# Attention and a squared-ReLU MLP on one core: the second half's output products regrouped by Strassen's scheme, with channels on the partitions

## Chip, cores and metric

One core of a Trainium2 chip. The metric is the device time of one execution in microseconds (us). All data is float32; inputs and outputs lie in DRAM.

## What is computed

Causal attention (4 batches, 12 heads, 448 positions, head width 64) gives x with 4 x 448 = 1792 tokens and 768 channels. Then follows an MLP without gates:

```
x   = softmax(mask(q k^T / 8)) v            # 1792 tokens x 768 channels
h   = max(x @ w_in, 0)                      # 768 -> 2048
out = (h * h) @ w_out                       # 2048 -> 768
```

The weights arrive as 8-byte floats and are turned into float32 on the chip.

## The kernel before

**Precision.** Every float32 factor is split into a high part `hi` (a copy in the format that TensorE reads) and a low part `lo = value - hi`. A product is three matmuls into one PSUM bank: hi*hi, hi*lo, lo*hi. A split is thus two instructions: `hi` by POOL or ACT (L305, L290), `lo` by DVE or POOL (L293, L297).

**Two phases.** Tokens 0 to 895 (batches 0 and 1) go first, tokens 896 to 1791 second. The attention of batches 0 and 1 opens the kernel; that of batches 2 and 3 is woven into phase 0's matmuls. In each phase the 2048 hidden channels come in 4 groups of 4 x 128. A group has an **h stage** (x @ w_in, ReLU, square) and an **o stage** (times w_out, added to an accumulator). In phase 0 the h stage is plain. Phase 0 loads the raw weights (`piece`), turns them into float32, splits them into the tiles `wi` and `wo`, and stores float32 copies in DRAM (`wz_dram` and `wo_dram`; `keep` also stores hi and lo of w_in for groups 0 and 3).

**Phase 1.** The h stage goes by Strassen's scheme with seven products (Winograd's form): the 896 tokens, the 768 channels and 256 hidden channels are each halved. `w_parts` loads the quarters of the weights, makes the sums s1 to s4 on DVE or POOL and splits them; `h_pair` runs 7 products x 3 channel blocks x 3 matmuls of 448 columns for each pair of hidden blocks (two pairs per group). The sums of x (t1 to t4) were put in DRAM by `spill` and come back by `x_part`. The o stage is plain (`o_unit`): tokens on the PSUM partitions, 14 units (7 token blocks x 2 column halves) of 4 x 3 matmuls of 384 columns, and one DVE addition each into `acc`. For groups 2, 1 and 0 `fetch` reads w_out back from `wo_dram` and splits it; group 3's is still there from phase 0. The groups go 3, 2, 1, 0 in phase 1; in the last one each unit of `acc` is stored as it is done.

**Order of the work.** A planner (`Plan.emit`) lists all operations with estimated costs and starts, at each step, the one that can start earliest; each operation names the engines that may do it, with a `BIAS` in us against some. What comes out is a fixed order for each engine: PE, ACT, DVE, POOL, and the DMA queue of SP. Each of them runs strictly in that order, so an instruction that waits holds up everything behind it on its engine. Buffers are pools (`plan.pool`): `f` for float32 scratch, `w` for split weights of phase 1, `r` for hidden values, `ps` for the eight PSUM banks. `lend` makes other tiles part of a pool once their first use is over.

Lines that matter below: L804 to L806 the plain o stage's matmuls, L743 to L747 the h stage's of phase 1, L616 to L618 of phase 0, L820 the addition into `acc` (issued by L293), L823 the store of the result.

Of the kernel before, what the change touches and what calls it, by code (L numbers as in the profile page):

```python
# [20 lines left out]
class Op:  # L21
    __slots__ = ("rank", "ways", "then", "left", "ready", "take", "drop", "lag")
# [14 lines left out]
class Plan:  # L37
# [8 lines left out]
    BIAS = {PE: 0.0, ACT: 0.5, DVE: 1.0, POOL: 0.0, DMA: 0.0, DMA2: 0.0}  # L46

    def __init__(self):
        self.ops, self.writer, self.readers = [], {}, {}
        self.pools, self.caps, self.held = {}, {}, {}  # L50

# [45 lines left out]
    def emit(self):  # L97
# [72 lines left out]
def kernel(  # L170
# [51 lines left out]
    NRAW, NZ, NB, NR = 3, 3, 1, 6  # L222
    CB = NP // 2
# [20 lines left out]
    def tiles(nm, n, shape, dtype, pool=const):  # L244
# [17 lines left out]
    plan.pool("r", tiles("r", NR, [P, S], F32), r=2, xs=4, y=6)  # L262
    plan.pool("f", [], fz=5, s=3, xp=3, fo=2)
    spare = [whole[:, i * S:(i + 1) * S].bitcast(F32) for i in range((2 * NRAW + NZ + NB) * PCW // S)]
    lent_f = plan.lend("f", spare)
# [4 lines left out]
        for i in range(2 * GF)] + [lambda i=i: late["w"][i] for i in range(2)])  # L270
# [4 lines left out]
    plan.pool("ps", tiles("ps", 8, [P, 512], F32, psum), mm=2, sc=4, pt=2, av=1, st=5)  # L275
# [23 lines left out]
    pool_too = [True]  # L299

    def two_sources(*args):
        return [on_dve(*args, 0.03) + SHARED] + ([on_pool(*args)] if pool_too[0] else [])
# [5 lines left out]
    def split(rank, n, hi, lo, src, reads, key, after=(), drop=(), take=None):  # L308
# [3 lines left out]
        plan.op(rank, two_sources(n, lo, src, lambda: hi().bitcast(F32), ALU.subtract),  # L312
                list(reads) + [(key, 0)], [(key, 1)], after, drop=drop)
# [162 lines left out]
    def spill(n, av, at):  # L476
# [27 lines left out]
        elif second:  # L504
# [6 lines left out]
            less(x12, [av])  # L511
# [13 lines left out]
    wo_dram = nc.dram_tensor("wo_whole", (NG, 2 * GF, P, CH), F32, kind="Internal").ap()  # L525

# [9 lines left out]

    def fetch(rank, gr, a, ch):
        h = Hold("f", "fo")
        plan.op(rank - 6, [(DMA, 0.9, lambda: nc.sync.dma_start(
            out=h.t[:, :CH], in_=wo_dram[gr, a + GF * ch]))], [("wod", gr, a, ch)], [h], take=h)  # L540
        cols = slice(ch * CH, (ch + 1) * CH)
        split(rank - 2, CH, lambda: late["wo"][:, 0, a, cols], lambda: late["wo"][:, 1, a, cols],
              lambda: h.t[:, :CH], [h], ("wo", a, ch), drop=[h])
# [3 lines left out]
    def piece(rank, kind, gr, a, ch, after):  # L547
# [88 lines left out]
    SEVEN = ("11", "s2", "12", "s3", "s1", "22", "s4")  # L636
# [21 lines left out]
    ahead = []  # L658

    def w_parts(gr, u, rank, last):  # L660
# [36 lines left out]
        else:  # L697
            for m, (key, f, j) in enumerate((("21", 1, 0), ("22", 1, 1), ("11", 0, 0), ("12", 0, 1))):
                Z[key] = h = Hold("f", "fz")
                plan.op(rank - 10 + m, [(DMA, 0.7, lambda h=h, f=f, j=j: nc.sync.dma_start(  # L700
                    out=h.t[:, :CBW].rearrange("p (c n) -> p c n", n=P), in_=wz_dram[gr, 2 * u + f, j]))],
                    [("wzd", gr, CB * j + c) for c in range(CB)], [h], gate, take=h)
        Z["s1"], Z["s2"], Z["s4"] = Hold("f", "s"), Hold("f", "s"), Hold("f", "s")
        Z["s3"] = Z["21"]

        def done(key):
            W[key] = w = Hold("w", "w")
            split(at(key), CBW, lambda: flat(w.t[:, 0]), lambda: flat(w.t[:, 1]), lambda: Z[key].t[:, :CBW],
                  [Z[key]], w, (), [Z[key]], take=w)

        def made(key, a, b, op, drop):
            combine(rank, CBW, Z[key], Z[a], Z[b], op, [Z[a], Z[b]], [Z[key]],
                    take=Z[key] if key != "s3" else None, drop=[Z[d] for d in drop])
        def direct(key):
            if gr not in (0, NG - 1):
                done(key)
        direct("11")
        made("s1", "21", "22", ALU.add, ("22",))
        made("s2", "s1", "11", ALU.subtract, ("s1", "11"))
        done("s2")  # L720
        direct("12")
        made("s3", "11", "21", ALU.subtract, ("11",))
        done("s3")
        done("s1")
        direct("22")
        made("s4", "12", "s2", ALU.subtract, ("12", "s2"))
        done("s4")
        ahead[:] = plan.ops[-2:]
        return W

    def h_pair(u, W, rank, step):

# [35 lines left out]
        product("s2", "b", True)  # L768
        add("u2", "b", "u2", False, [bank["b"]])
# [3 lines left out]
        squared(f1, 0, y["11"], rank)  # L773
        product("s3", "d", True)
        add("u3", "d", "u2", True, [])
        product("s1", "c", True)
        add("u3", "c", "u3", False, [])
        relu("u3")
        squared(f2, 1, y["u3"], rank)
# [3 lines left out]
        squared(f2, 0, y["21"], rank)  # L783
# [3 lines left out]
        squared(f1, 1, y["12"], rank)  # L787
        return rank

    def o_unit(ph, gr, t, ch, rank, step, after):  # L790
# [23 lines left out]
        first, final = (0, NG - 1) if ph == 0 else (NG - 1, 0)  # L814
        if gr == first:
# [14 lines left out]
    stack = ExitStack()  # L830
# [13 lines left out]
    def group(ph, gr, rank, step, begin):  # L844
# [7 lines left out]
        else:  # L852
            mid = (begin + rank) / 2
            W = [w_parts(gr, 0, begin, mid), w_parts(gr, 1, mid, rank)]
# [11 lines left out]
        else:  # L866
            for u in range(2):
                rank = h_pair(u, W[u], rank, H_US * step)
        for i in range(2 * GF):
            at = begin + (rank - begin) * (i + 0.5) / 8  # L870
            if ph == 0:
                piece(at, "o", gr, i % GF, i // GF, swap)
            elif gr < NG - 1:
                fetch(at, gr, i % GF, i // GF)
        begin = rank
        for ch in range(2):
            for t in range(NT):
                rank = o_unit(ph, gr, t, ch, rank, O_US * step, swap)
# [14 lines left out]
    def replace():  # L893
# [3 lines left out]
        late["w"] = tiles("w2_", 2, [P, 2, CB, P], F32R, pool)  # L897

    attended = over(plan.ops[mark:], lent_w[2 * GF:], replace)
    over(pieces, lent_f)  # L900
    entered = over(h_ops, lent_w[:2 * GF])
    keys = [(OTHER[key], i) for key in SEVEN for i in range(CB)]
    pool_too[0] = False
# [3 lines left out]
    for ph in range(1, NPH):  # L907
        for gr in range(NG - 1, -1, -1):
# [34 lines left out]
```

## Time and profile before

| | us |
|---|---|
| three runs | 624.04, 625.79, 626.65 |
| median | 625.79 |
| the profiled execution's own time | 624.94 |
| its span, first to last instruction | 623.2 |
| phase 1, from its first h matmul (at 399.21) | 224.0 of the span |

The profile is of one execution. "Busy" is the time in which an engine ran an instruction; matmuls overlap, so the distance between the starts of matmuls tells more than the duration of one. PEld is the loading of weights, which runs beside the matmuls. The granted clock is a share of TensorE's 2.4 GHz.

### The profile page before, as it was taken

What the parts mean: (1) busy time and instruction counts of PE and PEld (TensorE: products, weight loads), DVE (VectorE), ACT (ScalarE), POOL (GpSimd) and SP (SyncE); (2) the same over time, 40 slices, a digit from 0 to 9 for tenths busy, and PEclk for the clock granted to TensorE, in tenths of its full rate; (3) what the DMA queues carried; (4) which work ended last, traced back from release to release, by engine and by line L of the source; (5) the groups of instructions that cost most, each with busy time, mean ns of one, the idle gap of its engine ahead of it and who ended that gap; (6) DMA issues with size and microseconds to landing.
All of it is one profiled execution on the core that took longest, in us unless ns stands there. A gap on an engine that the chain in (4) does not pass through costs nothing.

```text
span 623.2 us, 11325 instructions
## 1 busy us (share of the span) xinstructions
PE 601.2 (96%) x3864; PEld 528.9 (85%) x3864; DVE 410.9 (66%) x932; ACT 306.0 (49%) x768; POOL 312.0 (50%) x427
## 2 busy tenths in 40 slices
PE   3989999999999999999999999999999999999997
PEld 2656677789988898888898889999999999999997
DVE  5779866478774789765977517886159646845432
ACT  4778987768667747585466540043235004202400
POOL 1457784568788756876655653452135222213100
PEclk9899999999999999999999999999999999999999
DMA  8888844689895679676875529832121203310022
GB/s 149 169 202 152 168 121 73 144 271 251 214 220 178 161 220 251 179 196 201 234 199 182 171 82 345 265 106 74 50 64 52 63 14 102 122 57 1 1 90 88
DMA packets 166314, 91.68 MB, mean 147 GB/s; under 512 B 115440, under 2 KB 157552, under 8 KB 166256
## 3 DMA queue, kind: packets, MB, share of 16 engines
q1 hardware_dynamic: 162544, 90.50, 54.1%
q10 hardware_dynamic: 3712, 0.46, 0.5%
q8 instruction: 30, 0.49, 0.3%
q14 instruction: 28, 0.23, 0.1%
HBM read 64.19 MB, written 26.74 MB: 146 GB/s over the span
## 4 chain that ended last, share of the span: by engine, by line
PE 83%; DVE 6%; DMA 4%; ACT 3%; POOL 1%; issue 1%; SPq 0%; ACTq 0%; DVEq 0%; POOLq 0%
PE ps L804 12%; PE ps L806 12%; PE ps L805 11%; PE ps L616 6%; PE ps L427 6%; PE ps L617 6%; PE ps L618 6%; PE ps L407 5%; PE ps L743 5%; PE ps L745 5%; PE ps L747 5%; PE ps L367 4%; DVE ps L380 2%; ACT ap L384 1%; POOL ap L393 1%
## 5 line engine op out<-in xcount | busy, mean ns | idle before, releaser
L804 PE MATMUL ps<-wo,g 128*128 128x384 f32 x448 | 151.7, 339 | 0.0
L806 PE MATMUL ps<-wo,g 128*128 128x384 f32 x448 | 150.1, 335 | 1.1 <-DVE g L293 1.1
L805 PE MATMUL ps<-wo,g 128*128 128x384 f32 x448 | 149.9, 335 | 0.0
L393 POOL TENSOR_SCALAR ap<-ap,asm 128x128 f32<-128x128 f32 (+6 forms) x122 | 78.2, 660 | 50.4 <-DVE asm L452 29.3
L290 ACT ACTIVATE r<-ps 128x448 f32<-128x448 f32 x60 | 32.7, 547 | 139.1 <-PE ps L747 108.4
L290 ACT ACTIVATE words<-words 128x384 f32<-128x384 f32 (+3 forms) x112 | 66.7, 613 | 52.0 <-DVE words L293 10.9
L806 PEld LDWEIGHTS ps<-wo,g 128*128 128x128 f32 x448 | 84.1, 188 | 1.4 <-DVE g L293 1.4
L804 PEld LDWEIGHTS ps<-wo,g 128*128 128x128 f32 x448 | 84.1, 188 | 1.3 <-issue 0.8
L805 PEld LDWEIGHTS ps<-wo,g 128*128 128x128 f32 x448 | 84.1, 188 | 0.2
L293 DVE TENSOR_TENSOR acc<-ps,acc 128x384 f32<-128x384 f32 x84 | 46.3, 554 | 55.7 <-PE ps L806 55.3
L380 DVE CUSTOM_DVE_ANT_0 ps<-ps,mask 128x448 f32<-128x448 f32 (+6 forms) x168 | 68.6, 444 | 18.9 <-PE ps L367 10.1
L616 PE MATMUL ps<-x,wi 128*128 128x448 f32 x192 | 74.8, 390 | 1.2 <-ACT x L290 0.6
L305 POOL TENSOR_SCALAR wo<-words 128x384 fp32r<-128x384 f32 x44 | 27.1, 621 | 88.1 <-PE ps L806 66.0
L617 PE MATMUL ps<-x,wi 128*128 128x448 f32 x192 | 70.2, 366 | 0.2 <-DVE x L293 0.2
L618 PE MATMUL ps<-x,wi 128*128 128x448 f32 x192 | 70.1, 365 | 0.0
L384 ACT ACTIVATE ap<-ps,mx 128x448 f32<-128x448 f32 (+6 forms) x126 | 58.3, 481 | 10.3 <-DVE mx L380 8.3
L305 POOL TENSOR_SCALAR g<-r 128x448 fp32r<-128x448 f32 x50 | 32.0, 642 | 53.5 <-ACT r L290 52.8
L290 ACT ACTIVATE r<-r 128x448 f32<-128x448 f32 x75 | 43.2, 578 | 30.0 <-DVE r L293 28.7
L293 DVE CUSTOM_DVE_ANT_0 words<-words 128x768 uint16<-128x768 uint16 (+1 forms) x56 | 45.4, 810 | 13.5 <-ACT words L290 10.5
L305 POOL TENSOR_SCALAR wi<-words 128x384 fp32r<-128x384 f32 (+1 forms) x43 | 28.0, 654 | 44.2 <-DVE words L585 15.4
L743 PE MATMUL ps<-x,wi 128*128 128x448 f32 x135 | 49.6, 368 | 0.4 <-DVE r L293 0.4
L745 PE MATMUL ps<-x,wi 128*128 128x448 f32 x135 | 49.5, 367 | 0.0
(83 smaller groups left out, 1139.5 us busy)
## 6 DMA issues: line engine op xcount, KB each, us to landing
words<-in_moe_w_in_dram SPq DMA_DIRECT2D x24, 512.0 KB, 4.6
words<-in_moe_w_out_dram SPq DMA_DIRECT2D x32, 384.0 KB, 3.8
wi_split<-wi SPq DMA_DIRECT2D x24, 256.0 KB, 3.6
out_dram<-acc SPq DMA_DIRECT2D x28, 192.0 KB, 3.2
v<-in_v_dram SPq DMA_DIRECT2D x24, 192.0 KB, 3.9
wo_whole<-words SPq DMA_DIRECT2D x24, 192.0 KB, 4.2
wi_whole<-words SPq DMA_DIRECT2D x18, 256.0 KB, 4.5
words<-wi_whole SPq DMA_DIRECT2D x24, 192.0 KB, 2.8
```

Source lines behind the costliest of these rows:

```text
L290: return (ACT, t_act(n, psum, more), lambda: nc.scalar.activation(dst(), src(), func, **kw))
L293: return (DVE, t_dve(n) + more, lambda: nc.vector.tensor_tensor(out=dst(), in0=a(), in1=b(), op=op))
L305: return (POOL, t_pool(n), lambda: nc.gpsimd.tensor_scalar(dst(), src(), 1.0, 1.0, op0=ALU.mult, op1=ALU.mult))
L380: plan.op(at, [(DVE, t_dve(w), lambda: nc.vector.tensor_tensor_reduce(out=at_(), in0=at_(), in1=mask[:, S - w:], scale=-SCALE, scalar=3.0e ...
L393: (POOL, 0.00083 * CW[c] + 0.3, lambda: nc.gpsimd.tensor_scalar(*operands(), 1.0, op0=ALU.mult, op1=ALU.mult)),
L616: nc.tensor.matmul(o, w[:, 0], x[:, 0], start=c == 0, stop=False)
L617: nc.tensor.matmul(o, w[:, 0], x[:, 1], start=False, stop=False)
L618: nc.tensor.matmul(o, w[:, 1], x[:, 0], start=False, stop=c == NP - 1)
L743: nc.tensor.matmul(o, w.t[:, 0, c], x[:, 0], start=begin and c == 0, stop=False, skip_group_check=True)
L804: nc.tensor.matmul(res(), g[:, 0], w[:, 0], start=f == 0, stop=False)
L805: nc.tensor.matmul(res(), g[:, 0], w[:, 1], start=False, stop=False)
L806: nc.tensor.matmul(res(), g[:, 1], w[:, 0], start=False, stop=f == GF - 1)
```

## The change

The o stage of phase 1 is turned: output channels lie on the PSUM partitions and 448 tokens are the columns. For the groups 0, 3 and 2, which come first (the order is now 0, 3, 2, 1), it uses the seven products; group 1, the last, is plain in the turned form. For this:

- `h_pair` makes the sums of the squared hidden values (t1 to t4) and splits seven factors instead of four per pair, into tiles of pool `g7` (12 tiles). Its products come in another order (11, 12, s3, s1, s2, 22, s4). ReLU and square are on ACT alone, a factor's `lo` on DVE alone.
- 15 running sums of 128 x 448 (`late["sum"]`) take the place of `acc`; the last group adds its product, transposes 32 x 32 blocks on DVE and stores the result in pieces of 32 channels (128 bytes) by four DMAs per tile, from SP or ACT.
- The sums of weights (s1 to s4, for the o stage of the three groups, and for the h stage of the groups 3, 2, 1) are made by DMAs that add: `added_up` loads a quarter, and POOL issues DMAs that add others onto it, with copies that change the sign in between, on POOL or ACT. The h stage of group 0 still adds on DVE or POOL.
- Phase 0 stores `wo` for all four groups (32 instead of 24 stores of 192 KB), and hi and lo of 26 of the 32 pieces in `wh_dram` (384 KB each).
- When phase 0 and the attention are over, the memory of `wo` and `acc` is used for g7, sums and scratch (`grow`). The pool `w` has 9 tiles instead of 10 and now serves both stages. From then on the bias against DVE is 0.3 instead of 1.0, against ACT 0 instead of 0.5, and POOL may again do operations with two sources.

```diff
-    BIAS = {PE: 0.0, ACT: 0.5, DVE: 1.0, POOL: 0.0, DMA: 0.0, DMA2: 0.0}
+    FEW = {PE: 0.0, ACT: 0.5, DVE: 1.0, POOL: 0.0, DMA: 0.0, DMA2: 0.0}
+    MANY = {PE: 0.0, ACT: 0.0, DVE: 0.3, POOL: 0.0, DMA: 0.0, DMA2: 0.0}
...
+    HWAY, OWAY, GWAY = slice(None), slice(1, 2), slice(0, 1)
+    TURNS, LEAD = (0, 3, 2, 1), 9
...
-    plan.pool("f", [], fz=5, s=3, xp=3, fo=2)
+    plan.pool("f", [], fz=5, xp=3, oz=12, tr=3)
...
-        if kind == "o" and gr < NG - 1:
+        if kind == "o":
             plan.op(rank, [(DMA, 0.8, lambda: nc.sync.dma_start(out=wo_dram[gr, a + GF * ch], in_=zf()))],
                     [zt], [("wod", gr, a, ch)], drop=[zt])
+            if (a % 2, ch) != (0, 1) or gr == TURNS[-1]:
+                plan.op(rank + 12, [(DMA, 1.2, lambda: nc.sync.dma_start(
+                    out=wh_dram[gr, a + GF * ch],
+                    in_=late["wo"][:, :, a, ch * CH:(ch + 1) * CH].bitcast(F32)))],
+                    [(key, i) for i in range(2)], [("whd", gr, a, ch)])
...
-    SEVEN = ("11", "s2", "12", "s3", "s1", "22", "s4")
+    SEVEN = ("11", "12", "s3", "s1", "s2", "22", "s4")
...
+        def added(h, key, at):
+            src, saved = source(key)
+            plan.op(at, [(POOL, 1.1, lambda: nc.gpsimd.dma_start(
+                out=shaped(h.t[:, :n]), in_=src, accum_op=ALU.add))], saved, [h])
+            plan.op(at, [(DMA, 0.7, lambda: None)], [], [h])
...
+        b = loaded("11", rank - 16)
+        a = loaded("21", rank - 14)
+        if not kept:
+            done("11", b, False)
+        derived(b, -1.0, b, rank - 13)
+        added(b, "21", rank - 12)
+        c = derived(b, 1.0, at=rank - 9)
+        done("s3", c)
+        added(a, "22", rank - 8)
+        done("s1", a)
+        added(b, "22", rank - 8)
+        d = derived(b, -1.0, at=rank - 5, drop=[b])
+        done("s2", b)
+        added(d, "12", rank - 4)
+        done("s4", d)
+        if not kept:
+            done("12", loaded("12", rank - 5))
+            done("22", loaded("22", rank - 3))
...
+        less("11", "12", "11")
+        factor("t1", "11", True)
+        less("12", "12", "u3")
+        factor("t3", "12", True)
+        less("u3", "u3", "11")
...
+        factor("t2", "u3", True)
+        less("21", "21", "u3")
...
+        factor("t4", "21", True)
...
+    def o_seven(gr, W, rank, step):
+
+        bank = {}
+        for key in SEVEN:
+            b, k, begin = O_BANK[key], O_SUM[key], key not in ("12", "22", "s4")
+            for d in range(CB):
+                if begin:
+                    bank[b, d] = Hold("ps", "os")
+                ps = bank[b, d]
+                rank = o_product(ps, [(W[key, u], g7[OTHER[key], u]) for u in range(2)], d, begin, True, rank, step)
...
+                if gr == TURNS[0] and key not in ("s1", "s2"):
+                    ways = [on_act(S, a, src, True)]
+                else:
+                    ways = [on_dve(S, a, src, a, ALU.add)]
...
+    def o_last(W, rank, step):
+
+        for k in ("11", "21", "12", "22"):
+            i, j = k
+            for d in range(CB):
+                ps, a = Hold("ps", "os"), o_sum(k, d)
+                rank = o_product(ps, [(W[i + m, u], g7[m + j, u]) for m in "12" for u in range(2)],
+                                 d, True, True, rank, step)
+                plan.op(rank, [on_dve(S, a, lambda ps=ps: ps.t[:, :S], a, ALU.add)], [ps], [("sum", k, d)], drop=[ps])
+                h = Hold("f", "tr")
+                plan.op(rank, [(DVE, t_dve(S) + 0.05, lambda h=h, a=a: nc.vector.transpose(h.t, a()))],
+                        [("sum", k, d)], [h], take=h)
...
+                            out=out[row:row + S, col + s * SQ:col + (s + 1) * SQ].rearrange(
+                                "(b p) d -> p b d", p=SQ),
+                            in_=h.t[s * SQ:(s + 1) * SQ].rearrange("p (b d) -> p b d", d=SQ))
+                    plan.op(rank, [(DMA, 0.6, go(nc.sync)), (DMA2, 0.6, go(nc.scalar))], [h], [], drop=[h])
...
-        for gr in range(NG - 1, -1, -1):
+        for gr in TURNS:
```

`o_product` runs, for one PSUM bank, three matmuls of 448 columns (hi*hi, hi*lo, lo*hi) for each pair of a weight tile and a factor tile: two pairs in `o_seven`, four in `o_last`. The weights' splits of the o stage have their `lo` on POOL alone (`OWAY`).

## Rows read from the trace of the kernel before

**Rows 1.** The page's first part: busy time, share of the span, instructions.

```profile
PE 601.2 (96%) x3864; PEld 528.9 (85%) x3864; DVE 410.9 (66%) x932; ACT 306.0 (49%) x768; POOL 312.0 (50%) x427
```

**Rows 2.** Windows: us, busy PE, PEld, DVE, ACT, POOL; clock, DMA share, GB/s.

```profile
100.00:200.00 100.00, 98.85 (x689) 84.50 (x683) 65.05 (x146) 71.30 (x179) 74.67 (x90) 1.00 0.74 195
200.00:300.00 100.00, 98.24 (x645) 86.44 (x642) 75.15 (x174) 62.56 (x155) 70.10 (x82) 1.00 0.73 197
399.21:619.80 220.59, 220.16 (x1177) 210.96 (x1176) 128.16 (x217) 53.38 (x97) 58.64 (x91) 1.00 0.22 69
```

**Rows 3.** PE's timeline: first matmuls of stages in phase 1, and the last.

```profile
399.21 0.37 PE L743 MATMUL ps<-x,wi 128*128 128x448 f32 x1
...
424.94 0.34 PE L804 MATMUL ps<-wo,g 128*128 128x384 f32 x1
...
454.09 0.37 PE L743 MATMUL ps<-x,wi 128*128 128x448 f32 x1
...
565.30 0.37 PE L743 MATMUL ps<-x,wi 128*128 128x448 f32 x1
...
590.48 0.34 PE L804 MATMUL ps<-wo,g 128*128 128x384 f32 x1
...
619.45 0.34 PE L806 MATMUL ps<-wo,g 128*128 128x384 f32 x1
```

**Rows 4.** Groups of instructions by shape: busy us, mean ns, idle before and releaser.

```profile
L293 DVE TENSOR_TENSOR r<-ps,r 128x448 f32<-128x448 f32 x40 | 24.8, 621 | 20.8 <-PE ps L747 20.6
L293 DVE TENSOR_TENSOR g<-r,g 128x448 fp32r<-128x448 f32 x38 | 26.1, 696 | 4.8 <-POOL g L305 4.8
L293 DVE TENSOR_TENSOR w<-words,w 128x384 fp32r<-128x384 f32 x8 | 4.4, 548 | 0.0
L290 ACT ACTIVATE r<-r 128x448 f32<-128x448 f32 x75 | 43.2, 578 | 30.0 <-DVE r L293 28.7
L290 ACT ACTIVATE r<-ps 128x448 f32<-128x448 f32 x60 | 32.7, 547 | 139.1 <-PE ps L747 108.4 <-PE ps L618 13.4 <-DVE r L494 8.1
L290 ACT ACTIVATE g<-r 128x448 fp32r<-128x448 f32 x14 | 8.0, 569 | 0.1
L290 ACT ACTIVATE wi<-words 128x384 fp32r<-128x384 f32 x7 | 3.7, 523 | 1.7 <-PE ps L745 1.7
L297 POOL TENSOR_TENSOR wo<-words,wo 128x384 fp32r<-128x384 f32 x30 | 32.4, 1085 | 1.2 <-ACT wo L290 0.3
```

**Rows 5.** Waits of PE after 400 us: total, times, longest.

```profile
PE ps L743 <- DVE r L293: 0.4, 1, 0.4
```

**Rows 6.** DMA issues: count, KB each, median us from issue to landing.

```profile
words<-wi_whole SPq DMA_DIRECT2D x24, 192.0 KB, 2.8
out_dram<-acc SPq DMA_DIRECT2D x28, 192.0 KB, 3.2
aq<-in_q_dram SPq DMA_DIRECT2D x68, 56.0 KB, 2.5
wi<-wi_split SPq DMA_DIRECT2D x9, 384.0 KB, 3.4
```

**Rows 7.** The tiles of k: ns of one issue and of one transpose (min/median/max).

```profile
L330 SPq DMA_DIRECT2D ak<-in_k_dram x72: 311/477/1712, 0.7 to 316.1; - x72
L348 DVE STREAM_TRANSPOSE akt<-ak x18: 635/640/647, 5.6 to 335.0; 128x448 f32<-128x448 f32 x18
```

**Rows 8.** The end: the last addition in the timeline.

```profile
619.83 0.56 DVE L293 TENSOR_TENSOR acc<-ps,acc 128x384 f32<-128x384 f32 x1 [1.53 <-PE ps L806]
```

**Rows 9.** Windows before phase 1 and at the start, columns as in rows 2.

```profile
380.00:390.00 10.00, 10.00 (x59) 10.00 (x58) 7.32 (x13) 0.00 (x0) 3.23 (x6) 1.00 0.99 359
390.00:400.00 10.00, 10.00 (x59) 9.95 (x58) 7.93 (x15) 0.00 (x0) 4.73 (x8) 1.00 0.85 270
...
4.00:5.00 1.00, 0.00 (x0) 0.00 (x0) 0.00 (x0) 0.00 (x0) 0.00 (x0) 1.00 1.46 162
```

More of the change, by code (lines that the diff above doesn't have):

```diff
@@ L269 @@
         wide[:, i * 2 * CBW:(i + 1) * 2 * CBW].rearrange("p (i c f) -> p i c f", i=2, c=CB)
-        for i in range(2 * GF)] + [lambda i=i: late["w"][i] for i in range(2)])
+        for i in range(2 * GF)] + [lambda: late["w"]])
     for t in v_t:
@@ L510, in spill @@
                     [t1], [x21])
-            less(x12, [av])
+            plan.op(at, [(DVE, t_dve(S) + 0.05, lambda: nc.vector.tensor_tensor(
+                out=x12.t, in0=x12.t, in1=result(), op=ALU.subtract))], [av], [x12], drop=[av])
             stored(t1, *t_place(2))
@@ L697, in w_parts @@
         else:
[L698 to L703, printed above, removed]
@@ L717, in w_parts, with source @@
[L717 to L727, printed above, removed]
+            where = {"11": (0, 0), "12": (0, 1), "21": (1, 0), "22": (1, 1)}
+            def source(key):
+                f, j = where[key]
+                return wz_dram[gr, 2 * u + f, j], [("wzd", gr, CB * j + c) for c in range(CB)]
@@ new lines, in done, with made @@
+        def done(key, h, last=True):
+            W[key] = w = Hold("w", "w")
+            split(at(key), CBW, lambda: flat(w.t[:, 0]), lambda: flat(w.t[:, 1]), lambda: h.t[:, :CBW],
+                  [h], w, gate, [h] if last else [], take=w, ways=HWAY)
+        if gr == 0:
+            def made(key, a, b, op, into):
+                Z[key] = Z[into]
+                other = a if into == b else b
+                combine(rank, CBW, Z[into], Z[a], Z[b], op, [Z[other]], [Z[into]])
+            made("s1", "21", "22", ALU.add, "22")
+            made("s3", "21", "11", ALU.subtract, "21")
+            begun[:] = plan.ops[-2:]
+            done("s3", Z["s3"])
+            done("s1", Z["s1"])
+            made("s2", "s1", "11", ALU.subtract, "11")
+            plan.ops[-1].drop = [Z["s1"]]
+            Z["s1"].drops += 1
+            done("s2", Z["s2"])
+            made("s4", "12", "s2", ALU.subtract, "12")
+            plan.ops[-1].drop = [Z["s2"]]
+            Z["s2"].drops += 1
+            done("s4", Z["s4"])
+        else:
+            added_up(rank, CBW, source, done, lambda t: t.rearrange("p (c n) -> p c n", n=P), gr == NG - 1)
@@ L772, in h_pair @@
                 take=y["11"], drop=[bank["a"]])
-        squared(f1, 0, y["11"], rank)
+        square("11")
+        factor("11", "11", plain)
         product("s3", "d", True)
-        add("u3", "d", "u2", True, [])
+        plan.op(rank, [on_act(S, lambda: y["u3"].t, out("d"), True)], [bank["d"]], [y["u3"]], take=y["u3"])
         product("s1", "c", True)
         add("u3", "c", "u3", False, [])
+        product("s2", "b", True)
+        add("u2", "b", "u2", False, [bank["b"]])
+        plan.op(rank, two_sources(S, lambda: y["u3"].t, lambda: y["u3"].t, lambda: y["u2"].t, ALU.add),
+                [y["u2"]], [y["u3"]], drop=[y["u2"]])
         relu("u3")
-        squared(f2, 1, y["u3"], rank)
+        square("u3")
+        factor("22", "u3", plain)
         product("22", "d", False)
@@ L782, in h_pair @@
         relu("21")
-        squared(f2, 0, y["21"], rank)
+        square("21")
+        factor("21", "21", plain)
         product("s4", "c", False)
@@ L786, in h_pair @@
         relu("12")
-        squared(f1, 1, y["12"], rank)
-        return rank
-    def o_unit(ph, gr, t, ch, rank, step, after):
+        square("12")
+        if plain:
+            factor("12", "12", True)
+            return rank
+        less("11", "12", "11")
[3 more added lines that the diff above has]
+        less("u3", "u3", "11")
+        plan.ops[-1].drop = [y["11"]]
+        y["11"].drops += 1
+        factor("t2", "u3", True)
@@ new lines, in o_sum, with o_product, go @@
+    def o_sum(k, d):
+        return lambda: late["sum"][("u2", "11", "12", "21", "22").index(k) * CB + d]
+    def o_product(ps, pairs, d, begin, end, rank, step):
+        for m, (w, g) in enumerate(pairs):
+            def go(w=w, g=g, start=begin and m == 0, stop=end and m == len(pairs) - 1):
+                o = ps.t[:, :S]
+                nc.tensor.matmul(o, w.t[:, 0, d], g.t[:, 0], start=start, stop=False, skip_group_check=True)
+                nc.tensor.matmul(o, w.t[:, 0, d], g.t[:, 1], start=False, stop=False, skip_group_check=True)
+                nc.tensor.matmul(o, w.t[:, 1, d], g.t[:, 0], start=False, stop=stop, skip_group_check=True)
+            plan.op(rank, [(PE, 3 * t_mm(S), go)], [(w, 0), (w, 1), (g, 0), (g, 1)], [ps],
+                    take=ps if begin and m == 0 else None, drop=[w, g])
+            rank += step
+        return rank
```

184 lines of the change are left out of this document (127 added, 57 removed).

## The prediction

> **What bounds the kernel now.** I read the page's busy shares first: PE has 96%, the others 66% or less [rows 1]. A busy share is an average, so the windows came next. In phase 1, from 399.21 to 619.8, PE lacks 0.4 us of 220.6, DVE is busy for 58% of it, ACT and POOL for about a quarter, and the DMA share is 0.22 [rows 2]. The list of PE's waits agrees: a single wait of 0.4 us after 400 [rows 5]. The clock was granted in full, 2.4 GHz [rows 2]. So phase 1 costs what its matmuls cost, and three engines and the DMAs have room. The reader should see that there only fewer matmul columns can win, and that what is paid for them in other work is free only as long as PE stays fed. Then PE's timeline, by distances between starts: the first h stage (126 matmuls of 448 columns) goes from 399.21 to 424.94, 25.73 us or 0.2042 each; the last one from 565.30 to 590.48, 0.1998 each; the o stage between (168 matmuls of 384 columns) from 424.94 to 454.09, 29.15 us or 0.1735 each [rows 3].
>
> **Matmuls.** The o stage before: 4 groups x 168 = 672 of 384 columns, 4 x 29.15 = 116.6 us. After: three groups of 7 products x 3 channel blocks x 2 pairs x 3 = 126 of 448 columns, and one of 4 x 3 x 4 x 3 = 144. At 0.2042 these are 3 x 25.7 + 29.4 = 106.6 us: **10.0 us less**. At 0.1998 they are 104.3, or 12.3 less. I take 0.2042, the pace of the stage in which DVE was busiest, as the new stages will be. The last, plain group gains nothing.
>
> **Work for the other engines.** I count a full group (both stages by seven products, weights of both summed by DMAs: 51.5 us of PE) with durations from [rows 4]. DVE alone: 29 additions from PSUM x 0.621 and 14 low parts x 0.696, 27.7 us. ACT alone: 14 ReLUs and squares x 0.578 and 6 copies x 0.547, 11.4 us. POOL alone: 8 low parts x 1.085 and 16 issues of adding DMAs. DVE or POOL: 10 sums x 0.696 and 14 low parts x 0.548 in DVE's time, 14.6 us. ACT or POOL: 14 high parts x 0.569 and 34 high parts and sign copies x 0.523 in ACT's time, 25.7 us. The trace has no adding DMA. What POOL pays for issuing one is bounded below by SP's issue of a load, 0.48 [rows 7], and above by POOL being held until a load of that size has landed, 2.8 [rows 6]; I take 1.085, POOL's own time for adding two sources of that size [rows 4], as the instruction that the DMA replaces. Then POOL alone has 26.0 us, and all together 105.4 us, or 35.1 for each of three engines: 68% of 51.5. Phase 0 ran in that state: from 100 to 300 us the three engines were busy 69 and 70% on average, and PE lost 1.15 and 1.76 us in 100 [rows 2]. So for 209 us of new phase 1 I take 1.45%, 3.0 us in place of 0.4: **2.6 us more**. The ends are 0 and the POOL case below.
>
> **Latency of the sums.** A unit's chain is a load (2.8), a sign copy (0.5) and three additions one after the other. An addition lands no sooner than a load (2.8) and, reading its target as well, I allow twice that, 5.6, each after an issue of 1.1: 15 to 23 us [rows 4, 6]. It costs nothing if it begins a unit or two (12.9 us each) ahead; twelve tiles of kind `oz` at four to six per unit allow two, and nine weight tiles hold 9 x 9 x 0.2042 = 16.5 us of products. If that cover is gone, a unit waits up to 23 - 16.5 = 6.5 us.
>
> **Order of products.** "12" now follows "11" on the same bank and must wait for ACT's copy out of it, 0.547 [rows 4]. It costs nothing as long as the planner puts the three blocks of s3 between; without them 8 units x 0.55 = 4.4 us. Behind DVE's additions wait the low parts of the next factors, and behind those PE; at the change from h to o, "11" and "12" give 36 matmuls, 7.4 us, before s3 needs the last factor, whose chain of seven instructions of 0.55 to 0.7 takes about 5. I cost it at nothing.
>
> **DMAs.** Phase 0 issues 34 more stores from SP (26 x 384 KB, 8 x 192 KB: 11.8 MB), at 0.48 or less each [rows 7]. At 359 GB/s, the most that a window shows [rows 9], they need 33 us of all engines in 400, and raise the share there from 0.74 to 0.82 [rows 2]. That cover is thin only at the boundary, where the share is already 0.99 and 0.85 [rows 9] with the loads of x for phase 1. Group 3's share of the stores is 3.9 MB, 11 us at 359 GB/s. They are due in its o stage or before; the loads of weights for the first units get smaller by 0.8 MB. I take **0.5 us more**; ends 0 and 11. In phase 1 SP has some ten loads more to issue (74 for 64), 5 us in 224, and POOL's queue the 48 adding ones; the stores of the result are 48 for 14, on two queues.
>
> **The end.** Before, the last addition starts at 619.83 and takes 0.56, and a store follows; the span ends at 623.2 [rows 8]. Now come an addition of 0.621, a transpose of 0.640 and four DMAs on two queues, so one issue more, 0.48 [rows 4, 7]: 0.06 + 0.64 + 0.1 + 0.48 = 1.3, and 56 KB pieces land in 2.5 against 3.2 [rows 6], of which I count nothing. With a tenth for semaphores, **1.4 us more**; ends 0.7 and 4.
>
> **Sum.** 624.94 - 10.0 + 2.6 + 0.5 + 1.4 = 619.4 in the terms of the profiled execution, which is 0.85 below the median of the runs. Against the median that makes 620.3.
>
> **Rivals.** *POOL becomes the bound (slower).* Each issue of an adding DMA stops POOL, which in the o stage alone makes the weights' low parts; behind it wait the high parts of factors, behind those DVE, then PE. POOL has room for 51.5 - 35.1 = 16.4 us more per full group, or an issue of 2.1 us. At 2.8 it would be 62.5 us, 11 over, in two full groups 22: 642. Over the slower bound it goes from about 2.4 us per issue (32 issues x 0.3 = 9). For it: 48 issues in an order fixed with 1.1 each, and no row of such an issue. Against: POOL was busy 26% of phase 1 before. The Trainium skill (DMA: Bandwidth & Descriptors, SWDGE vs HWDGE vs iDMA) says that GpSimd writes the descriptors of such DMAs into SBUF itself, where DVE in a two-port mode locks it out; that is this rival's mechanism, and no row here shows it. By that page's fit (Anatomy of one DMA) 192 KB take 2.45 us as a whole; if all of it were POOL's, the estimate would be 620.3 + 32 x 0.35 = 631.5.
>
> *The output's small pieces bound the last group.* Each tile of 229 KB goes out in 128-byte pieces, one per 12 matmuls, 2.45 us: 94 GB/s. Loads of q and k in such pieces moved 162 GB/s with the share above 1 [rows 9]; no row has stores of them. At half that rate 2.75 MB need 34.0 us against 29.4: 4.6 more, 625, no change. At a third it is 21 more. The Trainium skill (DMA: Bandwidth & Descriptors, Specifications) says that below 512 B the engine reads, modifies and writes, which speaks against this change; no trace here shows it for stores. Taken as half the rate it gives the 625.
>
> *The boundary starts late.* If the stores of group 3 stand in front of x, phase 1 begins up to 11 us later: at most 631, half of it 625.
>
> *Everything hides.* No idle time, the better pace and the short end: 625.8 - 12.3 + 0.7 = 614.
>
> **How the numbers follow.** About 0.5%, 3.1 us, is what a measurement of this kernel can tell: faster is below 622.7, slower above 628.9. The forecast, with the case that everything hides, has 0.60, all of it faster. The output case has 0.11 (0.10 no change, 0.01 slower), the boundary 0.11 (0.10 and 0.01), POOL 0.18, slower. That makes 0.60, 0.20, 0.20. The range starts at 614, where everything hides, and goes to 631, the whole boundary loss; beyond lie most of the POOL case and the output at a third, under 0.2.
>
> **What would show it.** PE's timeline: seven-product o stages of 25 to 26 us, the last 29. Windows of phase 1: DVE, ACT and POOL nearer to 70%, PE losing 3 us. The waits of PE: if over 10 us stand behind low parts made by DVE or POOL, the second term is wrong; if POOL's idle time is put down to issue, it is the POOL rival. The end: 4.8 us after the last matmul; a DMA share near 1 in the last 30 us means the output rival. A first matmul of phase 1 later than about 400 means the boundary. The forecast is wrong if the o stages keep their pace and the time does not fall.

## The result, and the profile after

The changed kernel takes **630.19 us** (median of 8 runs, 628.13 to 631.88) against 626.22 (8 runs) for the kernel before: a ratio of 1.0065, 95% interval 1.0046 to 1.0085. It is slower by 4.0 us where 5.5 us less were forecast (620.3 against 625.79). The two profiled executions lie further apart than the medians: 631.88 us, the longest of its eight, against 624.94, with spans of 630.1 and 623.2. The 6.9 us between the spans are split up first.

The page of the changed kernel, its first part, and the DMA queue that only it has (packets, MB, share of 16 engines' span):

```profile
PE 596.7 (95%) x3714; PEld 512.8 (81%) x3714; DVE 429.3 (68%) x938; ACT 358.6 (57%) x874; POOL 380.4 (60%) x483
...
q0 software_dynamic: 6912, 9.44, 9.9%
```

PE has 150 matmuls less, as counted, and less busy time than in [rows 1], in a longer span. PE's timeline, first matmuls of stages and the last one, to be read beside [rows 3]:

```profile
402.74 0.37 PE L797 MATMUL ps<-x,wi 128*128 128x448 f32 x1
...
428.41 0.36 PE L922 MATMUL ps<-g,wi 128*128 128x448 f32 x1
...
457.95 0.37 PE L797 MATMUL ps<-x,wi 128*128 128x448 f32 x1
...
484.84 0.36 PE L922 MATMUL ps<-g,wi 128*128 128x448 f32 x1
...
510.38 0.37 PE L797 MATMUL ps<-x,wi 128*128 128x448 f32 x1
...
539.77 0.37 PE L922 MATMUL ps<-g,wi 128*128 128x448 f32 x1
...
569.84 0.36 PE L797 MATMUL ps<-x,wi 128*128 128x448 f32 x1
...
624.50 0.36 PE L924 MATMUL ps<-g,wi 128*128 128x448 f32 x1
```

- Phase 1 starts at 402.74 instead of 399.21: 3.5 us later.
- From its first to its last matmul it takes 221.8 us instead of 220.2. The seven-product o stage of the second group, 484.84 to 510.38, takes 25.5 us, just what was forecast. But the first one takes 29.5, the third 30.1, and the h stage from 510.38 takes 29.4 instead of 25.7. An undisturbed distance between starts is 0.20 or 0.21 us. Distances of 0.44 us and more, less 0.20 each, add up to 8.8 us; those from 0.22 to 0.44 to 4.1. PE lost 12.9 us in phase 1.
- After the start of the last matmul come 5.6 us instead of 3.7.

3.5 + 1.5 + 1.9 = 6.9. Now where PE stood. Four stalls, at about 435, 446, 512 and 546, make 7.8 of the 8.8 us. Before the first, in the chain of work that ended last (start, us, what):

```profile
428.13 0.02 POOLq L678
...
428.15 6.70 DMA words<-wo_whole
...
434.94 0.18 ACT words L297
```

L678 is POOL's issue of an adding DMA. This one lands after 6.7 us; ACT, which runs in order, makes the sign copy of its sum, and only then the copy out of PSUM (`sa`) that PE waits for in the last of three gaps there. ACT itself stands for no more than 0.5 us for that landing; in the first two gaps PE waits for a high part by POOL and a low part by DVE. The stall at 512, with SP, POOL, ACT and PE in the timeline (start, us, engine, line, what, and the idle time before it with its releaser):

```profile
503.06 0.32 SPq L672 DMA_DIRECT2D words<-wo_whole  x1
...
508.55 0.86 POOL L678 DMA_DIRECT2D words<-wo_whole  x1 [4.52 <-DMA words<-wo_whole]
509.12 0.84 POOL L690 TENSOR_SCALAR words<-words 128x384 f32<-128x384 f32 x1
510.26 0.89 POOL L678 DMA_DIRECT2D words<-wo_whole  x1 [0.30 <-POOL words L690]
510.86 1.35 POOL L304 TENSOR_TENSOR w<-words,w 128x384 fp32r<-128x384 f32 x1
...
512.24 0.94 ACT L297 ACTIVATE words<-words 128x384 f32<-128x384 f32 x2 [4.57 <-POOL w L304]
513.08 0.92 ACT L297 ACTIVATE wi<-words 128x384 fp32r<-128x384 f32 x2
...
512.01 0.37 PE L801 MATMUL ps<-x,wi 128*128 128x448 f32 x1
513.64 0.47 PE L797 MATMUL ps<-x,wi 128*128 128x448 f32 x1 [1.25 <-ACT wi L297]
```

The addition at 508.55 goes onto a quarter that a plain load of SP brings, issued at 503.06: it lands after 5.4 us. POOL stands for 4.5 us, and behind it a sign copy, the next issues and a low part. ACT waits 4.6 us for that low part, and PE for ACT's high part. Windows of that time, for the DMAs and then for the clock (us, busy of the five engines, clock, DMA share, GB/s):

```profile
505.00:506.00 1.00, 1.00 (x7) 0.93 (x6) 0.87 (x3) 0.00 (x0) 0.00 (x0) 1.00 0.91 129
...
512.00:513.00 1.00, 0.38 (x2) 0.00 (x1) 0.00 (x0) 0.77 (x2) 1.00 (x2) 1.00 0.89 118
513.00:514.00 1.00, 0.36 (x2) 0.30 (x2) 0.33 (x1) 1.00 (x4) 0.98 (x3) 1.00 0.83 95
...
516.00:517.00 1.00, 1.00 (x4) 0.90 (x3) 0.00 (x0) 0.45 (x1) 0.97 (x2) 0.50 0.81 123
517.00:518.00 1.00, 1.00 (x4) 0.89 (x3) 0.00 (x0) 0.00 (x0) 0.62 (x1) 0.50 0.93 189
...
519.00:520.00 1.00, 1.00 (x7) 0.92 (x6) 0.56 (x1) 0.97 (x3) 0.00 (x0) 1.00 1.10 270
```

While the load is under way the DMAs are busy for 0.91 and move 129 GB/s, where 359 went with 0.99 in [rows 9]. And after these two us, in which PE was busy for a third, the granted clock falls to 0.50 (1.2 GHz) at 515.4 and is back at 518.8; from 515.5 to 518.5 matmuls start every 0.37 us instead of 0.20. The same follows the stall at 546, from 549.5 to 552.9. Each of these two costs about 1.6 us again in this way. The stalls at 435 and 446 do not: the clock stayed at 1.00 there.

The stall at 446, on DVE and POOL:

```profile
442.19 6.08 DVE L300 TENSOR_TENSOR g<-f,g 128x448 fp32r<-128x448 f32 x1
...
442.19 0.81 POOL L690 TENSOR_SCALAR words<-words 128x384 f32<-128x384 f32 x1
442.68 1.31 POOL L304 TENSOR_TENSOR wi<-words,wi 128x384 fp32r<-128x384 f32 x1
443.63 1.18 POOL L678 DMA_DIRECT2D words<-wo_whole  x1
444.26 2.58 POOL L304 TENSOR_TENSOR wi<-words,wi 128x384 fp32r<-128x384 f32 x2
446.19 1.48 POOL L678 DMA_DIRECT2D words<-wi_whole  x1
446.80 3.29 POOL L304 TENSOR_TENSOR wi<-words,wi 128x384 fp32r<-128x384 f32 x2
```

A low part that takes DVE 0.61 us elsewhere in this trace takes 6.08 while POOL works without a pause; PE waits for it 1.7 us. Its two sources and its target lie in SBUF, as those of POOL's operations. The Trainium skill (GPSIMD Engine Reference, Specifications) says that POOL shares its SBUF interfaces with DVE, with contention where DVE has two inputs in SBUF; the trace agrees, with these 6.08 us. At 546 PE waits 2.3 us for an addition from PSUM that stands behind a row of DVE operations without a pause from 538.65 to 547.7.

The adding DMAs land late. DMA issues of the changed kernel, those of weights (count, KB, median us from issue to landing):

```profile
words<-wo_whole POOLq DMA_DIRECT2D x22, 192.0 KB, 6.2
words<-wi_whole POOLq DMA_DIRECT2D x22, 192.0 KB, 4.5
...
words<-wi_whole SPq DMA_DIRECT2D x18, 192.0 KB, 3.9
words<-wo_whole SPq DMA_DIRECT2D x11, 192.0 KB, 5.2
```

Even the plain loads from SP take 3.9 and 5.2, against 3.1 and 3.0 in e7_plain_pool below, which has the same order without the additions (2.8 for `wi_whole` in [rows 6]): from 425 to 475 us the DMA share is 0.92 (first row of the windows below).

### The profile page after: what moved, and what is told of

Its sections match the earlier page's. It is cut to its first block, busy times and chain, and to the rows that moved or that the text cites. A ratio compares the mean times of both kernels' runs of the same rounds, so it can differ in the third digit from the quotient of the medians.

```text
span 630.1 us, 11422 instructions
## 1 busy us (share of the span) xinstructions
PE 596.7 (95%) x3714; PEld 512.8 (81%) x3714; DVE 429.3 (68%) x938; ACT 358.6 (57%) x874; POOL 380.4 (60%) x483
## 3 DMA queue, kind: packets, MB, share of 16 engines
q0 software_dynamic: 6912, 9.44, 9.9%
## 4 chain that ended last, share of the span: by engine, by line
PE 61%; DMA 13%; DVE 11%; ACT 5%; issue 4%; POOL 3%; SPq 3%; ACTq 0%; DVEq 0%; POOLq 0%
PE ps L995 5%; PE ps L432 5%; PE ps L997 5%; PE ps L996 5%; PE ps L922 4%; PE ps L923 4%; PE ps L924 4%; PE ps L620 4%; PE ps L412 4%; PE ps L372 4%; PE ps L801 4%; PE ps L797 4%; PE ps L799 4%; PE ps L621 4%; PE ps L622 4%
## 5 line engine op out<-in xcount | busy, mean ns | idle before, releaser
L297 ACT ACTIVATE words<-words 128x384 f32<-128x384 f32 (+3 forms) x136 | 78.9, 597 | 64.3 <-DMA words<-in_moe_w_out_dram 17.2
L398 POOL TENSOR_SCALAR ap<-ap,asm 128x128 f32<-128x128 f32 (+6 forms) x122 | 76.9, 650 | 47.2 <-DVE asm L457 30.3
L995 PE MATMUL ps<-wo,g 128*128 128x384 f32 x224 | 76.8, 343 | 0.0
L620 PE MATMUL ps<-x,wi 128*128 128x448 f32 x192 | 74.6, 389 | 0.7 <-ACT x L297 0.6
L997 PE MATMUL ps<-wo,g 128*128 128x384 f32 x224 | 75.1, 335 | 0.0
L996 PE MATMUL ps<-wo,g 128*128 128x384 f32 x224 | 75.1, 335 | 0.0
L304 POOL TENSOR_TENSOR wi<-words,wi 128x384 fp32r<-128x384 f32 (+1 forms) x53 | 68.9, 1348 | 3.0 <-ACT wi L297 1.3
L621 PE MATMUL ps<-x,wi 128*128 128x448 f32 x192 | 70.2, 366 | 0.2 <-DVE x L300 0.2
L622 PE MATMUL ps<-x,wi 128*128 128x448 f32 x192 | 70.1, 365 | 0.0
L922 PE MATMUL ps<-g,wi 128*128 128x448 f32 x162 | 60.0, 370 | 3.1 <-DVE sa L300 2.3
L923 PE MATMUL ps<-g,wi 128*128 128x448 f32 x162 | 59.8, 369 | 0.2 <-DVE g L300 0.2
L924 PE MATMUL ps<-g,wi 128*128 128x448 f32 x162 | 59.7, 368 | 0.0
L310 POOL TENSOR_SCALAR wi<-words 128x384 fp32r<-128x384 f32 (+1 forms) x44 | 30.7, 700 | 44.4 <-DVE words L584 16.6
L797 PE MATMUL ps<-x,wi 128*128 128x448 f32 x147 | 54.7, 372 | 2.1 <-ACT wi L297 1.3
L801 PE MATMUL ps<-x,wi 128*128 128x448 f32 x147 | 54.6, 372 | 0.2 <-DVE wi L300 0.2
L799 PE MATMUL ps<-x,wi 128*128 128x448 f32 x147 | 54.5, 371 | 0.0
L300 DVE CUSTOM_DVE_ANT_0 words<-words 128x768 uint16<-128x768 uint16 (+1 forms) x56 | 43.5, 777 | 11.6 <-ACT words L297 8.5
L412 PE MATMUL ps<-ident,ap 128*128 128x128 f32 x288 | 43.3, 283 | 7.9 <-POOL ap L398 7.3
L297 ACT ACTIVATE apt<-ps 128x512 f32<-128x512 f32 x71 | 38.7, 598 | 14.5 <-PE ps L412 14.4
```

Of the source, the lines that this page charges most:

```text
L297: return (ACT, t_act(n, psum, more), lambda: nc.scalar.activation(dst(), src(), func, **kw))
L620: nc.tensor.matmul(o, w[:, 0], x[:, 0], start=c == 0, stop=False)
L621: nc.tensor.matmul(o, w[:, 0], x[:, 1], start=False, stop=False)
L622: nc.tensor.matmul(o, w[:, 1], x[:, 0], start=False, stop=c == NP - 1)
L797: nc.tensor.matmul(o, w.t[:, 0, c], x[:, 0], start=begin and c == 0, stop=False, skip_group_check=True)
L801: nc.tensor.matmul(o, w.t[:, 1, c], x[:, 0], start=False, stop=c == CB - 1, skip_group_check=True)
```

## Experiments

All against the kernel before, timed on the same chip (626.2 to 626.7 there). "Phase 1" is the time from its first to its last matmul's start, "lost" what its distances of 0.22 us and more exceed 0.20 by, both from PE's timeline of one execution of each kernel. e3_nopool's is the longest of its ten (633.15 us).

| kernel | us | ratio, 95% interval | phase 1 | lost |
|---|---|---|---|---|
| changed | 630.19 | 1.0046 to 1.0085 | 221.8 | 12.9 |
| e1_stores | 626.25 | 0.998 to 1.001 | 219.8 | - |
| e2_sums | 620.22 | 0.988 to 0.993 | 211.9 | 3.6 |
| e3_nopool | 628.22 | 1.000 to 1.007 | 220.8 | 12.5 |
| e4_known | 637.97 | 1.015 to 1.022 | 228.3 | 19.9 |
| e5_sums_fixed | 619.89 | 0.986 to 0.992 | 212.0 | 3.3 |
| e6_sums_nopool | 627.95 | 1.000 to 1.005 | 218.3 | 9.6 |
| e7_plain_pool | 622.36 | 0.989 to 0.996 | 214.8 | 5.9 |
| e8_plain_sp | 617.24 | 0.982 to 0.990 | 209.0 | 0.5 |
| e9_adds_h | 623.21 | 0.993 to 0.996 | 216.0 | 7.1 |
| e10_adds_o | 620.52 | 0.988 to 0.994 | 212.9 | 4.1 |
| e11_sums_oway | 619.96 | 0.988 to 0.996 | 210.9 | 2.7 |

**e1_stores**: the late start. On the kernel before:

```diff
-        if kind == "o" and gr < NG - 1:
+        if kind == "o":
...
+            if (a % 2, ch) != (0, 1) or gr == 1:
+                plan.op(rank + 12, [(DMA, 1.2, lambda: nc.sync.dma_start(
+                    out=wh_dram[gr, a + GF * ch], ...))], ...)
```

> The kernel before with the new stores of phase 0 alone (26 of 384 KB, 8 of 192 KB; nothing reads the new 26). Theory S, the stores make phase 0 late: the first h matmul of phase 1 comes at about 402.7 instead of 399.2 and the time is 3 to 4 us above the kernel before. Rival, phase 0 lost its 3.5 us by the new order that the planner found for it: the time stays within 1 us of the kernel before.

626.25 against 626.32: theory S falls. The stores cost less than 0.9 us (the interval's upper end). In its own profile phase 1 starts at 401.7, 2.5 us later than in the kernel before's, though the times agree: the start of one execution tells little. In the profiles of eleven of the twelve kernels with these stores it lies between 398.6 and 402.7, 400.8 on average (e3_nopool's, at 405.0, is left out); the 3.5 us of the changed kernel are the top of that spread.

**e2_sums, e5_sums_fixed**: no adding DMA. On the changed kernel, in place of what `added_up` does, as e5_sums_fixed has it:

```diff
-        derived(b, -1.0, b, rank - 13)
-        added(b, "21", rank - 12)
...
-        added(d, "12", rank - 4)
-        done("s4", d)
+        c = loaded("22", rank - 12)
+        d = loaded("12", rank - 10)
+        sums(a, c, ALU.add, c, rank - 10)
+        done("s1", c)
+        sums(a, b, ALU.subtract, a, rank - 9)
+        done("s3", a)
+        sums(c, b, ALU.subtract, b, rank - 8, c)
+        done("s2", b)
+        sums(d, b, ALU.subtract, d, rank - 4, b)
+        done("s4", d)
```

> The changed kernel with every weight sum made by DVE or POOL from plain loads, no adding DMA. Theory A, the stalls of phase 1 (12.7 us, clock loss included) come from adding DMAs that land 5 to 6 us after their issue while POOL and ACT wait for them in order: stalls fall to 4 us or less and the time to about 622. Theory B, they come from DVE and POOL stretching each other's operations with two SBUF sources: 24 units' worth more of such operations make the stalls equal or longer, 630 to 636.

> As e2_sums (all weight sums by DVE or POOL from plain loads), with the buffers of s1 and s2 kept until they are split, which e2_sums did not do. The work is the same, so the time should be that of e2_sums within 2 us, 618 to 623, phase 1 about 212 us from its first to its last matmul, and the kernel faster than both.

In e2_sums two buffers were given back before their split had read them, so some factors are of other sums; the work is the same. `sums` is an operation on DVE or POOL. Theory A holds in this: the loss goes with the adding DMAs, for phase 1 takes 212 us and PE loses 3.3 to 3.6 without them. Whether they act by the waits for their landing or by the stretched operations of DVE, these two runs do not tell, since both are gone. e5_sums_fixed is faster than both kernels, by 1.1% against the kernel before (ratio 0.9892). Windows of the changed kernel, of e5_sums_fixed and of e7_plain_pool, in this order:

```profile
425.00:475.00 50.00, 47.25 (x227) 41.98 (x226) 33.67 (x43) 29.20 (x61) 39.51 (x46) 1.00 0.92 204
```

```profile
425.00:475.00 50.00, 48.45 (x230) 42.51 (x229) 44.19 (x65) 23.92 (x47) 27.33 (x29) 1.00 0.58 178
475.00:525.00 50.00, 50.00 (x248) 46.27 (x247) 41.48 (x68) 20.81 (x40) 31.57 (x35) 1.00 0.37 110
```

```profile
425.00:475.00 50.00, 49.66 (x241) 44.56 (x239) 30.39 (x46) 30.23 (x62) 32.21 (x44) 1.00 0.60 199
```

Without adding DMAs the DMA share falls from 0.92 to 0.58, POOL has 12 us less, DVE 10 us more, and PE is never out from 475 to 525. DVE is busy for 83% there. From 425 to 475, with DVE at 88%, PE is out for 1.6 us, 1.4 of them behind low parts of DVE.

**e3_nopool, e6_sums_nopool**: operations with two sources on DVE alone in phase 1, with and without adding DMAs.

```diff
-    HWAY, OWAY, GWAY = slice(None), slice(1, 2), slice(0, 1)
+    HWAY, OWAY, GWAY = slice(None), slice(0, 1), slice(0, 1)
...
-        return [on_dve(*args, 0.03) + SHARED, on_pool(*args)]
+        return [on_dve(*args, 0.03) + SHARED] + ([on_pool(*args)] if pool_too[0] else [])
...
     plan.bias = plan.MANY
+    pool_too[0] = False
```

> The changed kernel with all operations with two sources of phase 1 on DVE, as in the kernel before; adding DMAs kept. Theory A: stalls stay at 10 to 13 us, 628 to 632. Theory B: no DVE operation takes over 2 us any more, stalls fall to 5 us or less, 621 to 624. If DVE then has too much work, PE waits for DVE and the time is above 632.

> e5_sums_fixed with all operations with two sources of phase 1 on DVE. Theory B in its weak form (DVE and POOL still stretch each other without adding DMAs): 1 to 3 us less than e5_sums_fixed. Rival, DVE has too much then (over 45 of 51 us per full group): PE waits for it and the time is 2 to 8 us above e5_sums_fixed.

With adding DMAs, no DVE operation on the factors takes over 2 us any more (1.95 at most), and yet the time is far from theory B's 621 to 624: without the longest execution the median of e3_nopool is 627.6, 2.6 us below the changed kernel and within its own scatter (623.6 to 632.5). So theory B doesn't explain the whole. That the fuller DVE took back a part of the gain isn't ruled out: PE waits for it for 2.3 us there. Without adding DMAs the edit costs 8 us. e6_sums_nopool, one window, and what PE waits for after 400 us (total, times, longest):

```profile
475.00:525.00 50.00, 50.00 (x248) 46.28 (x247) 45.09 (x83) 19.95 (x38) 8.74 (x13) 1.00 0.36 108
...
PE ps L911 <- DVE g L300: 3.7, 2, 2.5
PE ps L910 <- DMA w<-wo_split: 2.3, 1, 2.3
```

In this window PE isn't out, with DVE at 90%; elsewhere it waits 3.7 us for DVE's low parts (1.4 in e5_sums_fixed), but also 2.3 for a load. That DVE is too full, as the rival said, accounts for a part of the 8 us; for the rest it isn't shown. POOL's operations with two sources are needed: with them the kernel without adding DMAs is 8 us faster, whatever they stretch.

**e4_known**: the planner counts more for the landing.

```diff
-            plan.op(at, [(DMA, 0.7, lambda: None)], [], [h])
+            plan.op(at, [(DMA, 0.7, lambda: None)], [], [h], lag=2.0)
```

> The changed kernel, only that the planner counts 2.0 us more for the landing of an adding DMA, near what the trace shows. Theory A: the fixed order then leaves POOL and ACT other work in the meantime, and 4 to 8 us of the stalls go: 622 to 627. Theory B: no change beyond 2 us, 628 to 632.

Both missed: 638. The other order put four low parts of POOL in a row behind two issues, and DVE came to lie beside them. DVE (the second operation of this piece takes 6.19 us) and POOL:

```profile
438.18 7.03 DVE L300 TENSOR_TENSOR g<-f,g 128x448 fp32r<-128x448 f32 x2
...
439.64 1.22 POOL L678 DMA_DIRECT2D words<-wo_whole  x1
440.24 4.48 POOL L304 TENSOR_TENSOR wi<-words,wi 128x384 fp32r<-128x384 f32 x4
```

PE lost 5.0 us in one gap there. A truer cost for the landing didn't help here: what stretches the operations isn't in the plan.

**e7_plain_pool, e8_plain_sp**: the same transfers without the addition, from POOL's queue and from SP's.

```diff
-                out=shaped(h.t[:, :n]), in_=src, accum_op=ALU.add))], saved, [h])
+                out=shaped(h.t[:, :n]), in_=src))], saved, [h])
```

```diff
-            plan.op(at, [(POOL, 1.1, lambda: nc.gpsimd.dma_start(
-                out=shaped(h.t[:, :n]), in_=src, accum_op=ALU.add))], saved, [h])
-            plan.op(at, [(DMA, 0.7, lambda: None)], [], [h])
+            plan.op(at, [(DMA, 0.7, lambda: nc.sync.dma_start(
+                out=shaped(h.t[:, :n]), in_=src))], saved, [h])
```

> The changed kernel with the 48 DMAs as plain loads from POOL's queue in the same places, order and buffers: the addition is left out, so the sums are not sums. Theory A1, the adding itself (slower packets, the target read as well) makes them land late: landing falls from 4.5 to 6.2 us to 3 or 4, the DMA share of 425 to 475 from 0.92 to 0.75 or less, stalls to 5 us or less, time 622 to 625. Theory A2, the issue from POOL and the waits in POOL's order are what costs: landing and stalls stay, 628 to 632.

> The same plain loads, again without the addition, issued by SP, so that POOL issues none. Both theories: stalls of 4 us or less and 619 to 623. If it is as slow as the changed kernel, the mere chain of loads that wait for sign copies is too long for the lead it has, and neither the adding nor POOL is the cause.

Theory A1 holds for the larger part: with the order as it was, the addition alone costs 630.2 - 622.4 = 7.8 us; the stalls like those at 435, 446 and 512 shrink to 0.5 us or less. PE still loses 5.9, not 5 or less. For A2 speak another 622.4 - 617.2 = 5.1: e8_plain_sp is faster than the 619 to 623 that both theories gave it. But there the planner's order changed too, so not all of this need be POOL's issues: the stall like that at 546 is still in e7_plain_pool (2.4 us at 534.6) and not in e8_plain_sp. e7_plain_pool, its queue, landings and issues (ns, min/median/max):

```profile
q0 software_dynamic: 3072, 9.44, 4.8%
...
words<-wo_whole POOLq DMA_DIRECT2D x22, 192.0 KB, 3.3
words<-wi_whole POOLq DMA_DIRECT2D x22, 192.0 KB, 3.1
...
L678 POOL DMA_DIRECT2D words<-wo_whole x22: 536/537/737, 415.1 to 502.9; - x22
```

The changed kernel, the issues of both stages:

```profile
L678 POOL DMA_DIRECT2D words<-wo_whole x22: 858/1088/2858, 419.3 to 513.6; - x22
L678 POOL DMA_DIRECT2D words<-wi_whole x22: 835/886/1477, 425.5 to 580.6; - x22
```

For the same 9.44 MB an addition needs 144 packets instead of 64 per DMA, twice the time of the DMA engines (9.9 and 4.8% of the span), 1.5 to 2 times POOL's time for an issue (0.89 and 1.09 against 0.58 and 0.54), and lands 1.4 to 2.9 us later.

**e9_adds_h, e10_adds_o**: adding DMAs for the sums of one stage alone, the other's as in e5_sums_fixed (`added_up` in `w_parts` and the version above in `o_parts`, or the other way).

> The changed kernel with adding DMAs for the sums of the h stage alone (24 of 48); those of the o stage by DVE or POOL as in e5_sums_fixed. If the loss goes with the number of adding DMAs, half of the 10 us is left: 624 to 626. If it comes from their bunching in groups that have 16 of them, less than a third is left: 620 to 623.

> The other half: adding DMAs for the sums of the o stage alone (24 of 48), where the low parts of the same weights are POOL's alone. By number 624 to 626; by bunching 620 to 623. If POOL's row of low parts behind a late sum is what stops DVE, as in the 6 us operation of the changed kernel, this half is the dearer one: 2 us or more above e9_adds_h.

24 adding DMAs in the h stage cost 623.2 - 619.9 = 3.3 us, 24 in the o stage 0.6; both together 10.3. e10_adds_o is in the range of the bunching, e9_adds_h just between the two ranges. The loss doesn't go with the number: two halves that cost 3.9 cost 10.3 together. That it is the sixteen in a group that cost so much fits this, but isn't shown, for each edit also gave another order. That the o stage's half is the dearer one falls.

**e11_sums_oway**: on e5_sums_fixed.

```diff
-    HWAY, OWAY, GWAY = slice(None), slice(1, 2), slice(0, 1)
+    HWAY, OWAY, GWAY = slice(None), slice(None), slice(0, 1)
```

> e5_sums_fixed with the low parts of the o stage's weights on DVE or POOL, whichever the planner has free, instead of POOL alone. If POOL's rows of these hold DVE up there too, 1 to 2 us less than e5_sums_fixed, 618 to 619; if DVE is the fuller engine (83 to 88% there), the same or up to 3 us more.

619.96 against 619.89: no difference that can be told.

## Why the prediction was wrong

**Matmuls**: right. Forecast 10.0 us less; e8_plain_sp, where PE loses half a us, has a phase 1 of 209.0 against 220.2: 11.2 less. With the loss that was forecast, phase 1 was to be 7.4 us shorter; in the changed kernel it is 1.5 longer.

**Latency of the sums**: this is the step that failed. "It costs nothing if it begins a unit or two ahead" looked at the chain and its buffers alone. It put the delay by the adding DMAs at nothing, and with them the kernel takes 10.3 us more (630.2 against 619.9 for e5_sums_fixed). The landings were not far from what I allowed: 4.5 us in the h stage, 6.2 in the o stage, against 5.6; a load took 3.9 and 5.2, against 2.8; and the chain has two sign copies, not one. But I had counted them in the chain of one unit, where they stand in the order of POOL and ACT. What is behind them there, sign copies, low and high parts of other weights, comes late with them: the stall at 512, and a part of that at 435. At 446 DVE is held for 6 us beside a row of POOL's issues and low parts. The step **Work for the other engines** took every operation at its length in the kernel before; in the changed one 29 of POOL's low parts of weights took 1.35 us on average, not 1.085. e5_sums_fixed loses 3.3 us, where 3.0 was forecast, and takes 619.9, where 620.3 was. That is in part luck: it has no issue of an adding DMA and other work on DVE than I counted, and its phase 1 is 0.9 us shorter than forecast, its start and its end 1.0 longer together. With adding DMAs the loss is 12.9.

**DMAs**: 34 more stores cost nothing that shows, near the 0.5 of the forecast; the boundary rival falls. What I left out is the DMAs' time for adding: the share from 425 to 475 went to 0.92, and 9.4 MB through the new queue took 62 us of all engines (9.9% of 630).

**The end**: 1.9 us more against 1.4. The output's small pieces don't bound: in 604 to 608 us they go out at 108 GB/s with a share of 0.66, and 44 of the 48 land in 2.0 and 2.3 us, the last four in 3.2 and 3.5. Two lines of DVE at the end, that window, and two of the kernel before, its last stores and its first loads:

```profile
624.89 0.62 DVE L300 TENSOR_TENSOR sb<-ps,sb 128x448 f32<-128x448 f32 x1 [1.12 <-PE ps L924]
625.55 0.65 DVE L969 STREAM_TRANSPOSE words<-sb 128x448 f32<-128x448 f32 x1
...
604.00:608.00 4.00, 4.00 (x21) 3.70 (x21) 1.71 (x4) 0.00 (x0) 0.00 (x0) 1.00 0.66 108
...
596.00:620.00 24.00, 23.79 (x138) 23.47 (x136) 6.31 (x12) 0.00 (x0) 0.00 (x0) 1.00 0.29 104
1.00:10.00 9.00, 3.18 (x32) 2.17 (x36) 3.78 (x15) 1.59 (x2) 1.84 (x7) 1.00 0.99 162
```

By proportion, 108 / 0.66 = 164 GB/s at full share (an estimate): not half of the 162 GB/s that loads, most of their packets of 128 bytes, moved with a share of 0.99. The Trainium skill (DMA: Bandwidth & Descriptors, Specifications) says that below 512 B the engine reads, modifies and writes; no halving against such loads shows here. But the small pieces do cost: at nearly the same rate the kernel before's stores, in pieces of 1536 bytes, took a share of 0.29, so the DMA time per byte is 2.2 times theirs.

**The POOL rival** had the right side and the right queue, but the wrong price. An issue takes 0.89 to 1.09 us, not 2.4, and POOL was busy for 55% of phase 1, not full. It was stopped by what it waits for (16.0 us for DMAs at L678 in the sum of its waits), and beside it DVE was stretched. The waits alone are not the loss: in e7_plain_pool POOL still waits 11.9 us for DMAs there, and PE loses 5.9 instead of 12.9.

Left open: why one DVE operation lasts through a whole row of POOL instructions with adding DMAs. The longest on the factors took 1.44 us where POOL issues no DMA (e5_sums_fixed, e8_plain_sp), 2.13 with plain issues (e7_plain_pool), 2.8 and 3.5 with half the adding ones (e9_adds_h, e10_adds_o), 6.08 with all; but 1.95 with all where POOL does no operation with two sources (e3_nopool). So an operation of 6 us showed only where adding DMAs and POOL's two-source operations came together (here and in e4_known, 6.19); each figure is one execution's longest. No run separates the issue from the order around it, and none divides the 10.3 us between the waits and the stretching.

## What to carry to other kernels

A DMA that adds is no free addition: here it cost its issue on POOL (about 1 us), twice the DMA time of a load, slowed the plain loads beside it (from 3.0 and 3.1 us to 5.2 and 3.9), and made engines that run in order wait for its landing, with everything behind it. Before work is moved to an engine that looks half idle, list what it will wait for, not only what it will do; here the same sums on DVE or POOL, though DVE was already the fullest engine but PE, were 10 us cheaper. A stall can cost as much again in clock: two of four stalls of 1.6 to 2.4 us were followed by 3.4 us at half the clock, 1.6 us of loss each.

## What was not expected

- 192 KB added by DMA: 144 packets instead of 64, 4.5 to 6.2 us to landing instead of 3.1 to 3.3.
- A DVE operation with two sources in SBUF, 0.61 us elsewhere, lasted 6.08 us beside a row of POOL instructions.
- Stores to DRAM in 128-byte pieces took no more DMA time than loads in mostly such pieces: by proportion 164 GB/s at full share, against 162 at 0.99.
- A forecast that fits the kernel without the edit's main device (620.3 and 619.9) was off by 10 us with it.
